# Where the running sums of a decode-attention gradient kernel lie in PSUM, and when its group preparation runs

## The chip, the cores and the metric

The kernel runs on one core of a Trainium2 chip. The metric is the device time of one execution in microseconds (us), taken as the median of several runs. Profiles are of one execution each.

## The reference

A decode step of a transformer block with one token, forward and backward. `x` is a row of 640 elements; it is normalised (`xn`), and attention and a gated MLP are added to it:

```python
x = A_x
xn = _layernorm(x, axis=-1)
return x + _A_ref(xn, A_k_cache, A_v_cache, A_wq, A_wo) + _B_ref(xn, B_w1, B_w3, B_w2)
# _A_ref: q = xn @ wq in 32 heads of 128; p = softmax(q k^T / sqrt(128)) over 8192 keys; (p v) @ wo
# _B_ref: (silu(xn w1) * (xn w3)) @ w2, with 1728 hidden elements
```

The outputs are this row and the gradients, for a given `grad_out`, of x, the K and V caches, wq, wo, w1, w3 and w2. All tensors are bf16. Each head has its own K and V of 8192 x 128, 2 MB each, and gradients dK and dV of the same size, which are outer products of a probability-like column with one row. So nearly all of the 303 MB that move are K and V in, dK and dV out.

## The kernel before

The order of the instructions on every engine is the order of the program text (a manual schedule). The waits between engines are added when the program is built, from which tiles each instruction reads and writes. The tiles of one pool and tag take turns in the buffers of that tag.

The MLP and its gradients come first. Then a loop over the heads (h from 0 to 30; the last head stands behind the loop) treats head c and the head after it, n, in one iteration. The heads lie in 8 groups of 4; `hh` is the place in the group, `g` the group. In one iteration VectorE (DVE) does, in this order:

- `product(n, "S", 0)`: K times q for half of the 128 columns, into a tile T (L403); TensorE (PE) sums T with eight matmuls by the identity into psS (L405);
- `probs(c)`: rZ, the reciprocal of the softmax's sum (L463), and the probabilities;
- `outer(c, ..., "V", 0)`: half of dV into a tile ot, mostly by VectorE (L425), 8 of the 32 columns of a half by ScalarE (ACT, L419);
- `row_dots(c)`, `product(n, "S", 1)`, the other half of dV, then `dscores(c)` (U2, L507) and half of dK;
- `row_max(n)`: reductions of psS (L446, L448);
- `product(n, "DP", 0)`: V times do, in the same manner as S, into psDP; then the other half of dK;
- `exps(n)`: negM, the negated maximum over all rows (L455), and behind it `product(n, "DP", 1)`;
- `weights(c)`: odq (L527), from the head's attention output and dq.

TensorE does the sums of T and several small things: mrow's matmul, which spreads the row maxima over all rows (L450, in `row_max`); `blocks_sum(c)`, eight f32 passes that gather a head's output and dq into two columns, od (L490); rsum's (L459) and rdot's (L503) column sums; on_ps, the group's collected outputs (L538); and the running sums of dxn (L541) and of out (L341, L658), which are added up over all heads.

Two PSUM tiles hold the small results. `accbank` is one tile for the whole kernel, with dxn in columns 0 to 4, out in 5 to 9, on_ps in 16 to 23 and od in 32 to 35. `sm` is a new tile in each head (`row_max`), in a pool with one buffer, with rsum's sum in column 3, rdot's in 4 and the maxima in 8 to 135. `finish_steps` lets ScalarE copy on_ps out (`on_cols`, L332). A third tile, dx_ps, takes dx of the MLP, in three parts of columns; each part is opened with a matmul that has the start flag.

The preparation of the next group, `prep_steps`, is a generator: it turns wo (L292, TensorE), copies it (woT, L297, ScalarE), and makes the broadcast rows q (`qs_g`) and do (`do_g`, L323) of four heads. `gap()` runs one step of the generator that is ahead in `steps`; there are four gaps in an iteration. The generator of the next group is appended at the end of a group's second iteration (hh 1), and the third (hh 2) ends with a fifth gap.

Loads go through SyncE's queue (SP), most stores through GpSimd's (POOL). [...]

Of the kernel before, what the change touches and what calls it, by code (L numbers as in the profile page):

```python
# [10 lines left out]
F32 = mybir.dt.float32  # L11
ALU = mybir.AluOpType
ACTF = mybir.ActivationFunctionType
AX = mybir.AxisListType
PSUM = bass.MemoryType.PSUM

P = 128
# [4 lines left out]
def kernel(  # L22
# [22 lines left out]
    nc = tc.nc  # L45
# [4 lines left out]
    F = B_w1.shape[1]  # L50
# [5 lines left out]
    GH = 4  # L56
# [46 lines left out]
    with tc.manual_schedule(engines=ORDERED):  # L103
# [29 lines left out]
        def turn_lanes(to):  # L133
            k = (to - dealt[0]) % LANES
            if k:
                rows = k if k > 1 else LANES + 1
                nc.gpsimd.dma_start(lane_pad[0:rows, dealt[1] % 2], wq_v[0:rows, 0:2, 0:8])
                dealt[:] = to % LANES, dealt[1] + 1

        def deal(dst, src, p0, p1):  # L140
            nc.gpsimd.dma_start(dst[p0:p1], src[p0:p1])
            dealt[0] = (dealt[0] + (LANES - 1 if p0 == 0 else P - p0)) % LANES
# [79 lines left out]
        nc.vector.memset(accbank[:, 0:16], 0.0)  # L222
        DXN0 = 0
        OUT0 = NC
        OP0 = 16
        OD0 = 32

        sel = consts.tile([P, P // GH], F32, name="sel")
        nc.vector.tensor_reduce(sel[:], ident_f[:].rearrange("p (q r) -> p q r", r=GH), AX.X, ALU.add)
# [50 lines left out]
        def prep_steps(g):  # L280
            G_ = grp[g]
            wq_g, wo_g = G_["wq"], G_["wo"]

            def bank(name, dt, pool=None, tag="w"):
                if g == 0 and pool is not None:
                    return pool.tile([P, GH * DH], dt, name=name, tag=tag)
                return ps_w.tile([P, GH * DH], dt, name=name, tag="w")

            def turn(ci):
                ps_t = bank("ps_t", BF16, ps_o, "ob")  # L290
                for hh in range(GH):
                    nc.tensor.transpose(ps_t[:, hh * DH:(hh + 1) * DH], wo_g[:, hh, ci * P:(ci + 1) * P], ident_bf[:])  # L292
                return ps_t

            def keep(ps_t):
                woT = wpool.tile([P, GH * DH], BF16, name="woT", tag="woT", bufs=3)
                nc.scalar.copy(woT[:], ps_t[:])  # L297
                return woT

            ps_q = bank("ps_q", F32, ps_s, "sm")  # L300
            for ci in range(NC):
                nc.tensor.matmul(ps_q[:], lhsT=xn_col_bf[:, ci:ci + 1].to_broadcast([P, P]), rhs=wq_g[:, ci, :],
                                 start=(ci == 0), stop=(ci == NC - 1))
            yield
            qs_g = wpool.tile([P, GH, DH], BF16, name="qs_g", tag="qs_g")
            nc.scalar.activation(qs_g[:].rearrange("p h d -> p (h d)"), ps_q[:], ACTF.Copy, scale=scale)
            G_["qs"] = qs_g
            ps_t = turn(0)
            yield
            woT = keep(ps_t)  # L310
            ps_t = turn(1)
            yield
            ps_d = bank("ps_d", F32, ps_acc, "acc")
            for ci in range(NC):
                nc.tensor.matmul(ps_d[:], lhsT=g_col_bf[:, ci:ci + 1].to_broadcast([P, P]), rhs=woT[:], start=(ci == 0), stop=(ci == NC - 1))
                if ci + 1 < NC:
                    woT = keep(ps_t)
                if ci + 2 < NC:
                    ps_t = turn(ci + 2)
                if ci not in (2, NC - 1):  # L320
                    yield
            do_g = wpool.tile([P, GH, DH], BF16, name="do_g", tag="do_g")
            nc.scalar.copy(do_g[:].rearrange("p h d -> p (h d)").rearrange("p (q r) -> p r q", r=GH),  # L323
                           ps_d[:].rearrange("p (r q) -> p r q", r=GH))
            G_["do"] = do_g
# [118 lines left out]
        def row_max(st):  # L444
            st.S = small.tile([P, J], F32, name="S_sb", bufs=1)
            nc.vector.tensor_reduce(st.S[:], st.ps["S"][:], AX.X, ALU.add)  # L446
            mrow = small.tile([P, 1], F32, name="mrow")
            nc.vector.tensor_reduce(mrow[:], st.S[:], AX.X, ALU.max)  # L448
            st.sm = ps_s.tile([P, 512], F32, name="sm", tag="sm")
            nc.tensor.matmul(st.sm[:, 8:8 + P], lhsT=mrow[:].to_broadcast([P, P]), rhs=ident_f[:], start=True, stop=True,  # L450
                             skip_group_check=True)

        def exps(st):
            negM = small.tile([P, 1], F32, name="negM")
            nc.vector.tensor_reduce(negM[:], st.sm[:, 8:8 + P], AX.X, ALU.max, negate=True)  # L455
            st.E = small.tile([P, J], F32, name="E", bufs=1)
            rsum = small.tile([P, 1], F32, name="rsum")
            nc.scalar.activation(st.E[:], st.S[:], ACTF.Exp, bias=negM[:], scale=1.0, accum_out=rsum[:])
            nc.tensor.matmul(st.sm[:, 3:4], lhsT=ones_f, rhs=rsum[:], start=True, stop=True, skip_group_check=True)  # L459

        def probs(st):
            rZ = small.tile([P, 1], F32, name="rZ")
            nc.vector.reciprocal(rZ[:], st.sm[:, 3:4])  # L463
            st.P2 = small.tile([P, J, 2], BF16, name="P2")
            nc.vector.tensor_scalar(st.P2[:], st.E[:].unsqueeze(2).to_broadcast([P, J, 2]), rZ[:], None, ALU.mult)
            st.Pf = small.tile([P, 2, ACT_J], F32, name="Pf")
            nc.scalar.activation(st.Pf[:], st.E[:].rearrange("p (a j) -> p a j", a=2)[:, :, JH - ACT_J:JH],  # L467
                                 ACTF.Copy, scale=rZ[:])
# [15 lines left out]

        def blocks_sum(st):
            c0 = OD0 + 2 * (st.h % 2)
            st.od = accbank[:, c0:c0 + 2]
            for r in range(WIDE):
                i, b = divmod(r, WIDE // 2)
                nc.tensor.matmul(st.od, lhsT=st.wide[i][:, b * DH:(b + 1) * DH], rhs=pick[:, r, :],  # L490
                                 start=(r == 0), stop=(r == WIDE - 1), skip_group_check=True)
# [6 lines left out]
        def row_dots(st):  # L498
            st.DP = small.tile([P, J], F32, name="DP_sb", bufs=1)
            nc.vector.tensor_reduce(st.DP[:], st.ps["DP"][:], AX.X, ALU.add)  # L500
            rdot = small.tile([P, 1], F32, name="rdot")
            nc.vector.scalar_tensor_tensor(st.S[:], st.DP[:], 1.0, st.P2[:, :, 0], ALU.mult, ALU.mult, accum_out=rdot[:])
            nc.tensor.matmul(st.sm[:, 4:5], lhsT=ones_f, rhs=rdot[:], start=True, stop=True, skip_group_check=True)  # L503

        def dscores(st):
            st.U2 = small.tile([P, J, 2], BF16, name="U2", bufs=1)
            nc.vector.scalar_tensor_tensor(st.U2[:], st.DP[:].unsqueeze(2).to_broadcast([P, J, 2]), st.sm[:, 4:5], st.P2[:],  # L507
                                           ALU.subtract, ALU.mult)
            st.Uf = None
            if st.h < H - 1:  # L510
                st.Uf = small.tile([P, 2, ACT_J], F32, name="Uf")
                nc.vector.tensor_copy(st.Uf[:], st.U2[:, :, 0].rearrange("p (a j) -> p a j", a=2)[:, :, JH - ACT_J:JH])  # L512
            wide_sums(st.K, st.U2, 1)
# [10 lines left out]
        def weights(st):  # L524
# [9 lines left out]
            om = small.tile([P, GH], F32, name="om")  # L534
            nc.scalar.activation(om[:], rmask[:], ACTF.Copy, scale=odq[:, 0:1])
            if hh == 0:
                G_["on_ps"] = accbank[:, OP0 + GH * (st.g % 2):OP0 + GH * (st.g % 2 + 1)]
            nc.tensor.matmul(G_["on_ps"][hh * (P // GH):(hh + 1) * (P // GH), :], lhsT=sel[:], rhs=om[:],  # L538
                             start=True, stop=True, skip_group_check=True)
            for ci in range(NC):  # L540
# [61 lines left out]
        def dx_part(wi, wt, c0, n):  # L602
            T = tpool.tile([P, n, F], BF16, name="T13", tag="T")
            nc.vector.tensor_tensor(T[:], wt[:, c0:c0 + n, :],
                                    bc_sb[:, wi, :].unsqueeze(1).to_broadcast([P, n, F]), ALU.mult)
            for i in range(F // DR1):
                nc.tensor.matmul(dx_ps[:, c0:c0 + n, :], lhsT=ident_bf[:], rhs=T[:, :, DR1 * i:DR1 * (i + 1)],  # L607
                                 start=(wi == 1 and i == 0), stop=(wi == 0 and i == F // DR1 - 1),
                                 skip_group_check=True)

        def grad(wi, wt):
# [82 lines left out]
        def gap():  # L694
            if steps and next(steps[0], "end") == "end":
                steps.pop(0)

        ob = ps_o.tile([P, 512], F32, name="ob", tag="ob")
        nc.tensor.matmul(ob[:], lhsT=ident_bf[:], rhs=zero_bf[:].to_broadcast([P, WIDE * DH]), start=True, stop=True)
        first = new_head(0)  # L700
# [16 lines left out]
        for h in range(H - 1):  # L717
# [7 lines left out]
            if prev:  # L725
                keep_dq(prev)
            gap()
            row_dots(c)
            attend(c)
            turn_wq(c)  # L730
# [24 lines left out]
            if h == H - 3:  # L755
                for by, dst, src in late:
                    by(dst, src)
                turn_lanes(0)
            gap()
            if n:  # L760
                exps(n)
                product(n, "DP", 1)
            weights(c)
            gap()
            if hh == 1 and g + 1 < NG:
                steps.append(prep_steps(g + 1))
            if hh == 2:
                gap()
            prev = c

        c = hs.pop(H - 1)
# [86 lines left out]
```

## Time and profile before

| | |
|---|---|
| median of 3 runs (lowest to highest) | 720.91 us (719.51 to 721.76) |
| the profiled execution's own time, its span | 720.1 us, 718.3 us |
| mean granted TensorE clock | 0.894 |
| DMA | 303.35 MB, mean 422 GB/s |
| GpSimd busy | 49.5 us (7%) |

On the profile page each engine's busy time stands with its share of the span. Forty equal slices of the span follow, with the busy share in tenths for each engine, the DMA engines' mean busy share and their GB/s. Groups of instructions are named by the line of the kernel, the engine and the operation, with output <- inputs; a bracket or the end of the row has the idle time before them, and what released them. PEld is TensorE's load of weights, which overlaps its matmuls. Matmul ends are modelled.

### The profile page before, as it was taken

The page shows a single profiled execution, that of the slowest core. Times are in us where ns is not written, and L with a number is a line of the kernel's source. Part 1 is how long each engine was busy: PE and PEld are TensorE (multiplying, and loading weights), DVE is VectorE, ACT ScalarE, POOL GpSimd, SP SyncE. Part 2 cuts the span into 40 slices and gives each one's busy share as a digit, 9 for nine tenths or more (in the row PEclk, how much of TensorE's full clock was granted, in tenths as well). Part 3 has the DMA queues.
Part 4 walks back from the last instruction along what each step waited for, and adds up shares of the span by engine and source line. Part 5 has one row for each costly group of instructions (what it writes and reads, how often), then busy time and mean ns, then how long its engine had stood idle before and what let it go on. Part 6 is the DMA issues. An engine that isn't in the chain of part 4 may idle for free.

```text
span 718.3 us, 10242 instructions
## 1 busy us (share of the span) xinstructions
PE 552.2 (77%) x3698; PEld 277.9 (39%) x3698; DVE 630.6 (88%) x722; ACT 479.3 (67%) x1455; POOL 49.5 (7%) x91
## 2 busy tenths in 40 slices
PE   5787788778888797787788787488887878777770
PEld 3653344334444343343343344143443334333330
DVE  5789999899999996798899899499998989999982
ACT  2166666796678856596577866468667957777552
POOL 0010000000000210000000110000000000000100
PEclk9699998997998988799899889889989899999995
DMA  8999999999999999999999999999999999999997
GB/s 354 414 428 425 430 429 430 390 428 428 432 430 429 429 425 426 428 427 429 432 431 428 430 427 424 429 428 427 431 432 428 429 430 430 428 430 431 429 423 309
DMA packets 27696, 303.35 MB, mean 422 GB/s; under 512 B 3264, under 2 KB 3974, under 8 KB 9982
## 3 DMA queue, kind: packets, MB, share of 16 engines
q1 hardware_dynamic: 13490, 154.89, 51.0%
q0 software_dynamic: 10960, 137.72, 45.1%
q10 hardware_dynamic: 3196, 10.10, 3.5%
q8 instruction: 29, 0.48, 0.2%
q14 instruction: 21, 0.17, 0.1%
HBM read 151.34 MB, written 151.34 MB: 421 GB/s over the span
## 4 chain that ended last, share of the span: by engine, by line
DMA 41%; DVE 28%; PE 22%; ACT 5%; issue 1%; SPq 0%; POOL 0%; DVEq 0%; ACTq 0%; POOLq 0%
DMA Kt<-in_A_k_cache_dram 24%; DVE T L403 14%; DMA out_dram<-ot 10%; DVE ot L425 8%; PE ob L474 5%; PE psS L405 5%; PE psDP L405 5%; DMA lane_pad<-in_A_wq_dram 4%; ACT ot L419 3%; DMA Vt<-in_A_v_cache_dram 3%; DMA dbc<-in_B_w_dram 2%; PE accbank L490 1%; DVE DP_sb L500 1%; DVE S_sb L446 1%; PE dx_ps L607 1%
## 5 line engine op out<-in xcount | busy, mean ns | idle before, releaser
L405 PE MATMUL psDP<-T,ident_bf 128*128 128x512 bf16 x512 | 152.2, 451 | 62.1 <-DVE T L403 61.9
L405 PEld LDWEIGHTS <-ident_bf 128*128 128x128 bf16 x1024 | 108.3, 109 | 199.9 <-issue 125.6
L419 ACT ACTIVATE ot<-qs_g,Uf 128x128 bf16<-128x128 bf16 x496 | 151.7, 393 | 41.9 <-DVE Uf L512 26.8
L403 DVE TENSOR_TENSOR T<-Kt,qs_g 128x4096 bf16<-128x4096 bf16 x64 | 146.3, 2286 | 17.4 <-DMA Kt<-in_A_k_cache_dram 16.9
L419 ACT ACTIVATE ot<-do_g,Pf 128x128 bf16<-128x128 bf16 x504 | 153.9, 389 | 1.1
L403 DVE TENSOR_TENSOR T<-Vt,do_g 128x4096 bf16<-128x4096 bf16 x64 | 146.0, 2282 | 2.9 <-ACT do_g L323 1.6
L405 PE MATMUL psS<-T,ident_bf 128*128 128x512 bf16 x512 | 130.2, 400 | 14.9 <-DVE T L403 14.0
L425 DVE TENSOR_TENSOR ot<-qs_g,U 128x3072 bf16<-128x3072 bf16 (+1 forms) x64 | 113.1, 1768 | 13.3 <-DMA out_dram<-ot 13.3
L425 DVE TENSOR_TENSOR ot<-do_g,P 128x3072 bf16<-128x3072 bf16 (+1 forms) x64 | 112.8, 1762 | 6.8 <-DMA out_dram<-ot 5.8
L432 POOL DMA_DIRECT2D out_dram<-ot x60 | 32.2, 537 | 549.9 <-DVE Uf L512 279.3
L474 PE MATMUL ob<-Kt,U 128*4 128x512 bf16 x512 | 60.5, 379 | 1.3 <-DVE U L507 1.3
L474 PE MATMUL ob<-Vt,P 128*4 128x512 bf16 x512 | 61.0, 381 | 0.0
L531 ACT ACTIVATE dq_diag<-ident_bf,odq 128x128 bf16<-128x128 bf16 x32 | 12.8, 401 | 47.2 <-DVE odq L527 47.2
L490 PEld LDWEIGHTS accbank<-pick,wide 128*128 128x128 f32 x256 | 40.1, 223 | 7.8 <-issue 2.4
L467 ACT ACTIVATE Pf<-E,rZ 128x16 f32<-128x16 f32 x32 | 9.8, 305 | 48.4 <-DVE rZ L463 48.4
L297 ACT COPY woT<-ps_t 128x512 bf16<-128x512 bf16 x40 | 23.0, 576 | 21.5 <-PE ps_t L292 21.5
L490 PE MATMUL accbank<-pick,wide 128*128 128x2 f32 x256 | 35.6, 261 | 0.5 <-ACT wide L482 0.5
L450 PE MATMUL sm<-ident_f,mrow 128*128 128x128 f32 x64 | 16.0, 334 | 23.5 <-DVE mrow L448 23.5
L474 PEld LDWEIGHTS <-U 128*4 128x4 bf16 x512 | 19.8, 84 | 36.7 <-DVE U L507 5.2
L474 PEld LDWEIGHTS <-P 128*4 128x4 bf16 x512 | 19.9, 84 | 25.4 <-issue 0.8
L446 DVE TENSOR_REDUCE S_sb<-psS 128x64 f32<-128x512 f32 x32 | 21.9, 685 | 6.0 <-PE psS L405 6.0
L482 ACT COPY wide<-ob 128x256 f32<-128x256 f32 x64 | 19.9, 360 | 8.9 <-PE ob L474 8.9
(165 smaller groups left out, 538.3 us busy)
## 6 DMA issues: line engine op xcount, KB each, us to landing
out_dram<-ot POOLq DMA_DIRECT2D x60, 2048.0 KB, 24.8
Kt<-in_A_k_cache_dram SPq DMA_DIRECT2D x32, 2048.0 KB, 26.4
Vt<-in_A_v_cache_dram SPq DMA_DIRECT2D x32, 2048.0 KB, 21.1
out_dram<-ot SPq DMA_DIRECT2D x8, 1024.0 KB, 13.3
out_dram<-wo_g ACTq DMA_DIRECT2D x6, 640.0 KB, 15.9
wo_g<-in_A_wo_dram ACTq DMA_DIRECT2D x6, 640.0 KB, 15.4
wq<-in_A_wq_dram SPq DMA_DIRECT2D x2, 1280.0 KB, 33.7
w1t<-in_B_w_dram SPq DMA_DIRECT2D x1, 2160.0 KB, 12.3
```

Source lines behind the costliest of these rows:

```text
L297: nc.scalar.copy(woT[:], ps_t[:])
L403: nc.vector.tensor_tensor(T[:], src[:, :, ds_], vec[:, ds_].unsqueeze(1).to_broadcast([P, J, DHH]), ALU.mult)
L405: nc.tensor.matmul(ps[:], lhsT=ident_bf[:], rhs=T[:, :, RUN * i:RUN * (i + 1)], start=(half == 0 and i == 0), stop=(half == 1 and i == DHH ...
L419: nc.scalar.activation(st.ot[half][:, JH - ACT_J + j].rearrange("p a b -> p (a b)"), vec, ACTF.Copy, scale=wf[:, half, j:j + 1])
L425: nc.vector.tensor_tensor(st.ot[half][:, 0:n], vec.rearrange("p (a b) -> p a b", b=2).unsqueeze(1).to_broadcast([P, n, DH // 2, 2]), w2[:, ...
L432: nc.gpsimd.dma_start(dst.rearrange("p j d -> p (j d)"), st.rows[:])
L446: nc.vector.tensor_reduce(st.S[:], st.ps["S"][:], AX.X, ALU.add)
L450: nc.tensor.matmul(st.sm[:, 8:8 + P], lhsT=mrow[:].to_broadcast([P, P]), rhs=ident_f[:], start=True, stop=True, skip_group_check=True)
L474: nc.tensor.matmul(ob[c0:c0 + WIDE, :], lhsT=w2[:, WIDE * q:WIDE * (q + 1), 0], rhs=src[:, WIDE * q:WIDE * (q + 1), :].rearrange("p j d -> ...
L482: nc.scalar.copy(part[:], ob[:, i * (WIDE // 2) * DH:(i + 1) * (WIDE // 2) * DH])
L490: nc.tensor.matmul(st.od, lhsT=st.wide[i][:, b * DH:(b + 1) * DH], rhs=pick[:, r, :], start=(r == 0), stop=(r == WIDE - 1), skip_group_che ...
L531: nc.scalar.activation(dq_diag[:], ident_bf[:], ACTF.Copy, scale=odq[:, 1:2])
```

## The change

The columns of od and on_ps move from `accbank` to `sm`, and `sm` becomes one tile for the whole kernel, allocated ahead of the loop. `accbank` keeps dxn and out alone. dx_ps is opened once, by the first matmul of its first part. In `prep_steps` the steps are cut elsewhere: the copy and matmuls of ci 2, 3 and 4 form the sixth step and the copy into do_g the seventh. The fifth gap moves from the end of the third iteration of a group to the fourth iteration, behind the first gap. The second group's preparation is appended one iteration sooner. A new function, `mark_lanes`, issues eight small loads on GpSimd's queue behind the last turn of the lanes.

```diff
+        def mark_lanes():
+            for i, n in enumerate((3, 5, 6, 7, 9, 10, 11, 12)):
+                r = STRIP + 2 * i
+                nc.gpsimd.dma_start(lane_pad[r:r + 2].rearrange("p a b c -> p (a b c)")[:, 0:n], wq_v[0:2, 0, 0:n])
...
         DXN0 = 0
         OUT0 = NC
-        OP0 = 16
-        OD0 = 32
+        Z0 = 0
+        DOT0 = 1
+        MAX0 = 8
+        OD0 = MAX0 + P
+        OP0 = OD0 + 4
...
-                if ci not in (2, NC - 1):
+                if ci not in (2, NC - 2):
                     yield
...
-            st.sm = ps_s.tile([P, 512], F32, name="sm", tag="sm")
-            nc.tensor.matmul(st.sm[:, 8:8 + P], lhsT=mrow[:].to_broadcast([P, P]), rhs=ident_f[:], start=True, stop=True,
+            nc.tensor.matmul(sm[:, MAX0:MAX0 + P], lhsT=mrow[:].to_broadcast([P, P]), rhs=ident_f[:], start=True, stop=True,
                              skip_group_check=True)
...
-            nc.vector.tensor_reduce(negM[:], st.sm[:, 8:8 + P], AX.X, ALU.max, negate=True)
+            nc.vector.tensor_reduce(negM[:], sm[:, MAX0:MAX0 + P], AX.X, ALU.max, negate=True)
...
-            st.od = accbank[:, c0:c0 + 2]
+            st.od = sm[:, c0:c0 + 2]
...
-                G_["on_ps"] = accbank[:, OP0 + GH * (st.g % 2):OP0 + GH * (st.g % 2 + 1)]
+                G_["on_ps"] = sm[:, OP0 + GH * (st.g % 2):OP0 + GH * (st.g % 2 + 1)]
...
-                                 start=(wi == 1 and i == 0), stop=(wi == 0 and i == F // DR1 - 1),
+                                 start=(wi == 1 and c0 == 0 and i == 0), stop=(wi == 0 and i == F // DR1 - 1),
...
+        sm = ps_s.tile([P, 512], F32, name="sm", tag="sm")
         ob = ps_o.tile([P, 512], F32, name="ob", tag="ob")
...
             gap()
+            if hh == GH - 1:
+                gap()
             row_dots(c)
...
                 turn_lanes(0)
+                mark_lanes()
...
-            if hh == 1 and g + 1 < NG:
+            if hh == (1 if g else 0) and g + 1 < NG:
                 steps.append(prep_steps(g + 1))
-            if hh == 2:
-                gap()
             prev = c
```

The sums of rsum and rdot change their columns in the same way (`Z0` and `DOT0` in place of 3 and 4).

## The prediction

> **What bounds the kernel now.** I read the page's slices first, then VectorE's waits, then the timeline of one head, then the same rows in a head where TensorE ran at half clock.
>
> The slices of the page:
> ```profile
> PE 552.2 (77%) x3698; PEld 277.9 (39%) x3698; DVE 630.6 (88%) x722; ACT 479.3 (67%) x1455; POOL 49.5 (7%) x91
> ...
> DMA  8999999999999999999999999999999999999997
> ```
> The DMA engines are full from the second slice to the last but one, and VectorE (DVE) is busy 88%. Two resources share the bound, so what matters is how often VectorE waits for DMA, since that is the slack in which a new VectorE wait costs nothing. From the waits of VectorE (us in total, times, longest):
> ```profile
> DVE ot L425 <- DMA out_dram<-ot: 19.1, 4, 10.1
> DVE T L403 <- DMA Kt<-in_A_k_cache_dram: 16.9, 12, 4.1
> DVE S_sb L446 <- PE psS L405: 6.0, 5, 2.0
> DVE odq L527 <- PE accbank L490: 5.2, 10, 1.2
> DVE T L403 <- ACT do_g L323: 1.6, 3, 0.6
> DVE T L403 <- DMA Vt<-in_A_v_cache_dram: 1.1, 2, 0.9
> ```
> DMA holds VectorE back for 19.1 + 16.9 + 1.1 = 37.1 us, 1.2 us for each of the 31 loop iterations. That is all the slack there is. Head 4 by the timeline (start, duration, engine and line; in brackets the idle time before, and who ended it):
> ```profile
> 148.81 2.28 DVE L403 TENSOR_TENSOR T<-Vt,do_g 128x4096 bf16<-128x4096 bf16 x1
> 151.01 1.75 DVE L425 TENSOR_TENSOR ot<-qs_g,U 128x3072 bf16<-128x3072 bf16 x1
> 151.15 1.89 PE L405 MATMUL psDP<-T,ident_bf 128*128 128x512 bf16 x8 [1.71 <-DVE T L403]
> 152.68 0.28 DVE L455 TENSOR_REDUCE negM<-sm 128x1 f32<-128x128 f32 x1
> 152.87 0.95 PE L490 MATMUL accbank<-pick,wide 128*128 128x2 f32 x8
> 152.88 2.28 DVE L403 TENSOR_TENSOR T<-Vt,do_g 128x4096 bf16<-128x4096 bf16 x1
> 155.08 0.15 DVE L527 TENSOR_TENSOR odq<-accbank,sc 128x2 f32<-128x2 f32 x1
> 157.09 0.23 PE L538 MATMUL accbank<-om,sel 128*32 128x4 f32 x2
> 157.54 0.16 DVE L463 RECIPROCAL rZ<-sm 128x1 f32<-128x1 f32 x1
> ```
> VectorE runs without a hole here: one head takes 18.7 us from reciprocal to reciprocal. Note that negM (152.68, from `sm`) starts before blocks_sum's matmuls (152.87, into `accbank`) have run. Head 5, the granted clock halved from 170.4 on:
> ```profile
> 169.87 3.06 PE L405 MATMUL psDP<-T,ident_bf 128*128 128x512 bf16 x8 [1.71 <-DVE T L403]
> 171.40 0.28 DVE L455 TENSOR_REDUCE negM<-sm 128x1 f32<-128x128 f32 x1
> 172.72 1.71 PE L490 MATMUL accbank<-pick,wide 128*128 128x2 f32 x8
> 174.71 3.57 PE L405 MATMUL psDP<-T,ident_bf 128*128 128x512 bf16 x8
> 178.32 0.27 PE L538 MATMUL accbank<-om,sel 128*32 128x4 f32 x2
> ```
> The same eight psDP matmuls take 3.57 us for 1.89, and blocks_sum ends 3.03 us after negM's start instead of 1.14.
>
> **The part that decides: od and on_ps move into `sm`.** The waits between engines are made from the program, by PSUM tile and not by column. The program of before has two such waits: ScalarE's copy of on_ps (L332) waits for the last of L541's matmuls, which writes other columns of `accbank`; and L538's matmul carries a wait for VectorE's read of od (L527), also other columns. The latter stands in the trace, one event in each head:
> ```profile
> L538 PEldq EVENT_SEMAPHORE  x32: 51/51/51, 77.3 to 700.0; - x32
> ```
> After the change mrow's matmul, od, rsum's sum, on_ps and rdot's sum are columns of one tile, so a read by VectorE waits for the last TensorE write into any of them that stands ahead of it in program order. By that order:
>
> 1. negM (L455) follows blocks_sum and must wait for it. Behind it in VectorE's queue stand T of the second DP half, odq, T of the next head: everything. Price: from negM's start to the end of L490's last matmul. Read off the timeline iteration by iteration, that is 1.14 us in 19 of the 31 and 2.26 to 3.54 us (mean 2.76) in 12, where the clock was halved or the step began late: 19 x 1.14 + 12 x 2.76 = 54.8 us. I add 0.03 us each time for the step between the engines (in head 5 L490 ends at 174.43 and odq, which waits for it, starts at 174.46), 0.9 us. The 5.2 us that odq waits for L490 today fall inside. Net 50.5 us.
> 2. rZ (L463) follows on_ps's matmul (L538) and must wait for it. At full clock L538 ends at 157.32, 0.22 us before rZ: hidden by T of the next head. At half clock psDP is 1.68 us longer, so the wait is about 1.68 - 0.22 = 1.46 us (in head 5 L538 ends at 178.59, 1.67 us after rZ). None in any head would be 0, all heads 31 x 1.46 = 45 us. Today L538 ends after rZ in 10 iterations, 15.3 us in sum. After the change TensorE idles longer between blocks_sum and the second DP half (2.3 us of negM and T, against 1.4 between 153.82 and 155.22 in head 4), which makes half clock there more frequent; I take 15 heads, 22 us.
> 3. odq (L527) must wait for rsum's matmul (L459). It ended before odq in most heads, and T (2.28 us) covers it: nothing; up to 3.2 us once, in head 10, where ScalarE was late.
> 4. rdot's matmul (L503) waits for ScalarE's on_cols (L332) in the first head of a group, behind eight ot copies of 2.45 us. Queued behind it is attend. VectorE has its own 1.75 us outer product in between; 7 heads, 0 to 0.5 us each, taken at nothing.
>
> `accbank`, left with sums that nothing reads until L804, costs nothing and gains nothing. Opening dx_ps once changes a flag on matmuls and no count.
>
> The Trainium skill, "PSUM — Partial Sum Buffer", "Summary: rules for kernel authors", says to read PSUM while a matmul runs only from a different bank; before keeps this rule for negM against blocks_sum, the change breaks it. By that rule alone the price is the same as under 1.
>
> **Preparation.** Today the fifth step directly follows the fourth at the end of a group's third head. ScalarE's in-order queue then stands 3.90 us at 116.23 for ps_t before Pf, and in the fourth head VectorE loses 1.71 us on S_sb (128.54) and 0.60 us on do_g. The move puts two steps with three 0.58 us copies and two sets of transposes (0.38 us) ahead of rdot instead; TensorE and ScalarE alternate there, some 0.5 us a turn. At most the whole 6.0 + 1.6 us of these waits goes; at worst U waits about 1 us more in 6 groups. I take -1 us. The second group a head sooner moves the same instructions to heads 1 and 2; no DMA moves, its wo was loaded at the start.
>
> **mark_lanes.** Eight DMA issues on GpSimd's queue behind the last lane_pad one at 670.4; at its 0.95 us each 7.6 us, on a queue that holds nothing afterwards. Like their forerunner (landing in 25.8 to 38.8 us) they land by about 717, before the end of 718.3. Nothing, with a bound of 1 us.
>
> **The sum.** VectorE's path gets 50.5 + 22 - 1 = 71.5 us longer. It gives back the 37.1 us of DMA waits, as DMA then has time to catch up, and part of the tail: the last K half is computed at 701.9 and the span ends 16.4 us later, since stores of 1 MB take 13.3 us to land behind a backlog; with an empty queue I estimate 6 us less. 71.5 - 37.1 - 6 = +28.4. The profiled execution took 720.1 us (span 718.3, 1.8 outside): 748.5, and the median of the runs lies 0.8 above it: **749 us**.
>
> **Rivals.**
> - *DMA hides it* (not slower). The slack of 1.2 us a head is just the full-clock price, 1.14 + 0.03. If TensorE stays at full clock in nearly all heads, DMA stays the bound: 720 to 727 us. It decides as long as VectorE's average loss is under about 1.2 us a head. For it: slices of 428 to 430 GB/s throughout. Against: 12 slow heads in 31. 0.10.
> - *No such waits* (the regrouping of PSUM does not add them, by columns being told apart). Then preparation alone is left: 719 us, since DMA hides most of it. Against: L332 and L538 above. 0.07.
> - *The clock feeds back.* More idle time, more half clock. If all heads went at half clock: 31 x 2.8 - 5 + 45 - 43 = +84, 804 us; half of that extra gives 777. For it: four of the first five half-clock stretches of the loop (91.92, 112.40, 170.43 and 228.45) begin within 1.4 us of the start of a first DP half, right behind an idle time of TensorE. Against: most stretches end within 7 us. 0.15 for over 770. The Trainium skill, "TensorE: Matmul & The Clock Gate", "Part 1: The HAM clock gate", says that an idle window of about 3.4 us halves the clock; the trace agrees on the length, since the stretches are multiples of 3.41 us (91.92 to 95.33), and shows them after partly idle windows too: the stretch from 112.40 follows 3.41 us in which psDP's matmuls had run since 111.06.
>
> **Numbers.** My case has 0.68, with its own range 735 to 770. The range 724 to 786 takes in part of the first rival and most of the third. 0.3%, or 2.2 us, is about what a measurement of this kernel can tell from no change; the second rival lies half on that line, the first mostly within or above. Faster 0.05, same 0.09, slower 0.86.
>
> **What would show it.** Right: in VectorE's waits a new row of negM for L490, about 50 us, in nearly every head; a row of rZ for L538, 10 to 35 us; the waits for out_dram and Kt under 10 us; DMA slices at 400 to 415 GB/s; no change in the matmul counts; eight more lane_pad issues. Wrong: no idle time before negM, or idle time there with the DMA slices still full and DMA waits still about 37 us.

## The result, and the profile after

The changed kernel takes 773.05 us (median of 4 runs, 768.90 to 777.51) against 720.21 us (719.36 to 721.76): ratio 1.073, interval 1.067 to 1.080. That is 53 us more; 749 was forecast, with a range of 724 to 786. The profiled execution of the changed kernel, the longest of the four, took 777.51 us; its span is 775.6 us, 57.3 us above the 718.3 of before. Its lines are renumbered: negM is L462 (was L455), blocks_sum L497 (L490), rZ L470 (L463), on_ps's matmul L545 (L538), T L411 (L403), psDP's and psS's matmuls L413 (L405), ot L433 (L425), rdot L510 (L503), on_cols L340 (L332).

The page's busy times, the granted clock, the DMA engines' slices and rates, and the shares of the chain that ended last:

```profile
PE 592.1 (76%) x3698; PEld 291.5 (38%) x3698; DVE 633.8 (82%) x722; ACT 480.9 (62%) x1455; POOL 53.6 (7%) x99
...
PEclk9689998879888779898889779998979779978795
DMA  8999989999989999999989999999989999999956
GB/s 355 420 422 433 424 323 387 396 373 387 410 326 416 420 407 425 409 423 428 430 325 419 419 392 420 414 428 427 426 341 411 414 385 388 363 406 373 407 232 238
...
DVE 56%; PE 36%; ACT 3%; issue 2%; DMA 2%; SPq 0%; DVEq 0%; ACTq 0%
```

The instruction counts of TensorE, VectorE and ScalarE are those of before, and VectorE does the same work (633.8 us for 630.6). But DMA has fallen from 41% to 2% of the chain that sets the end, and the rates have holes of 323 to 341 GB/s; over the loop they average 396, for 428 before (400 to 415 in the slices was forecast). The bound is now VectorE together with TensorE. VectorE's waits say where:

```profile
DVE negM L462 <- PE sm L497: 58.5, 31, 3.0
DVE rZ L470 <- PE sm L545: 42.8, 31, 3.5
...
DVE S_sb L454 <- PE psS L413: 3.4, 7, 2.0
DVE odq L534 <- PE sm L497: 3.2, 1, 3.2
```

Two rows that did not exist before, each in all 31 iterations, 101.3 us in sum. Every row with a wait for Kt, Vt or out_dram is gone: the 37.1 us of DMA waits were given back in full. The timeline of iteration 1, which answers to head 4 of before:

```profile
96.32 1.75 DVE L433 TENSOR_TENSOR ot<-qs_g,U 128x3072 bf16<-128x3072 bf16 x1
96.45 1.89 PE L413 MATMUL psDP<-T,ident_bf 128*128 128x512 bf16 x8 [1.71 <-DVE T L411]
...
98.17 0.95 PE L497 MATMUL sm<-pick,wide 128*128 128x2 f32 x8
...
99.16 0.29 DVE L462 TENSOR_REDUCE negM<-sm 128x1 f32<-128x128 f32 x1 [1.09 <-PE sm L497]
99.37 2.28 DVE L411 TENSOR_TENSOR T<-Vt,do_g 128x4096 bf16<-128x4096 bf16 x1
...
101.57 0.15 DVE L534 TENSOR_TENSOR odq<-sm,sc 128x2 f32<-128x2 f32 x1
101.71 3.38 PE L413 MATMUL psDP<-T,ident_bf 128*128 128x512 bf16 x8 [1.34 <-DVE T L411]
...
105.07 0.22 PE L545 MATMUL sm<-om,sel 128*32 128x4 f32 x2
...
105.33 0.17 DVE L470 RECIPROCAL rZ<-sm 128x1 f32<-128x1 f32 x1 [1.22 <-PE sm L545]
```

negM no longer starts beside blocks_sum but 0.04 us after its last matmul has ended (98.17 + 0.95 = 99.12). The first DP half ran at full clock (1.89 us), the second mostly at half clock (3.38 us). From the end of blocks_sum (99.12) to the start of the second half (101.71) TensorE stood idle for 1.95 us (0.61 and 1.34), against 1.01 (0.52 and 0.49) in head 4 of before; whether that is the reason, e9 tests below. So on_ps's matmul is late, and rZ waits 1.22 us for it. In iteration 8 both halves ran slowly:

```profile
250.97 3.06 PE L413 MATMUL psDP<-T,ident_bf 128*128 128x512 bf16 x8 [1.71 <-DVE T L411]
...
253.83 1.71 PE L497 MATMUL sm<-pick,wide 128*128 128x2 f32 x8
...
255.57 0.29 DVE L462 TENSOR_REDUCE negM<-sm 128x1 f32<-128x128 f32 x1 [2.99 <-PE sm L497]
...
258.12 3.57 PE L413 MATMUL psDP<-T,ident_bf 128*128 128x512 bf16 x8 [1.14 <-DVE T L411]
...
261.99 0.17 DVE L470 RECIPROCAL rZ<-sm 128x1 f32<-128x1 f32 x1 [1.47 <-PE sm L545]
```

An iteration takes 21.2 us in the first case and 23.4 in the second; head 4 of before took 18.7. By the timelines of all 31 iterations, half clock touches the first DP half in 15 of them (12 before) and the second in all 31 (12 before).

From the first rZ to the last the loop grew from 629.8 to 687.5 us, +57.6. The terms by VectorE's waits in the loop: 58.5 + 42.8 new; 37.1 of DMA, 4.0 of odq for L490, 2.7 of S_sb and 1.6 of do_g gone; +55.9. VectorE's own instructions take 3.1 us longer there (576.1 us for 573.0), and 1.4 us of smaller differences stay. The stretch ahead of the loop is 2.6 us longer, the one behind it 2.9 us shorter.

### The profile page after: what moved, and what is told of

Same layout as the page of the kernel before. It is cut to its first block, busy times and chain, and to the rows that moved or that the text cites. A ratio compares the mean times of both kernels' runs of the same rounds, so it can differ in the third digit from the quotient of the medians.

```text
span 775.6 us, 10248 instructions
## 1 busy us (share of the span) xinstructions
PE 592.1 (76%) x3698; PEld 291.5 (38%) x3698; DVE 633.8 (82%) x722; ACT 480.9 (62%) x1455; POOL 53.6 (7%) x99
## 3 DMA queue, kind: packets, MB, share of 16 engines
q1 hardware_dynamic: 13490, 154.89, 50.5%
## 4 chain that ended last, share of the span: by engine, by line
DVE 56%; PE 36%; ACT 3%; issue 2%; DMA 2%; SPq 0%; DVEq 0%; ACTq 0%
DVE T L411 26%; PE psDP L413 24%; DVE ot L433 17%; PE sm L497 4%; DVE S_sb L454 3%; DVE DP_sb L507 2%; ACT ot L427 2%; PE ob L481 2%; PE psS L413 2%; DMA dbc<-in_B_w_dram 2%; DVE negM L462 1%; DVE P L472 1%; DVE U L514 1%; ACT woT L305 1%; PE dx_ps L614 1%
## 5 line engine op out<-in xcount | busy, mean ns | idle before, releaser
L413 PE MATMUL psDP<-T,ident_bf 128*128 128x512 bf16 x512 | 186.2, 530 | 88.7 <-DVE T L411 88.7
L413 PEld LDWEIGHTS <-ident_bf 128*128 128x128 bf16 x1024 | 114.5, 115 | 230.1 <-issue 170.2
L411 DVE TENSOR_TENSOR T<-Kt,qs_g 128x4096 bf16<-128x4096 bf16 x64 | 146.2, 2285 | 1.1 <-PE psDP L413 1.1
L411 DVE TENSOR_TENSOR T<-Vt,do_g 128x4096 bf16<-128x4096 bf16 x64 | 146.0, 2282 | 0.0
L413 PE MATMUL psS<-T,ident_bf 128*128 128x512 bf16 x512 | 126.6, 392 | 1.0 <-DVE T L411 1.0
L433 DVE TENSOR_TENSOR ot<-do_g,P 128x3072 bf16<-128x3072 bf16 (+1 forms) x64 | 112.9, 1763 | 1.1
L433 DVE TENSOR_TENSOR ot<-qs_g,U 128x3072 bf16<-128x3072 bf16 (+1 forms) x64 | 113.2, 1768 | 0.0
L462 DVE TENSOR_REDUCE negM<-sm 128x1 f32<-128x128 f32 x32 | 9.3, 291 | 58.5 <-PE sm L497 58.5
L538 ACT ACTIVATE dq_diag<-ident_bf,odq 128x128 bf16<-128x128 bf16 x32 | 12.9, 402 | 58.4 <-DVE odq L534 58.4
L465 ACT ACTIVATE E<-S_sb,negM 128x64 f32<-128x64 f32 x32 | 11.1, 348 | 59.9 <-DVE negM L462 59.8
L497 PEld LDWEIGHTS sm<-pick,wide 128*128 128x128 f32 x256 | 44.5, 246 | 9.0 <-issue 4.1
L470 DVE RECIPROCAL rZ<-sm 128x1 f32<-128x1 f32 x32 | 5.4, 168 | 42.8 <-PE sm L545 42.8
L497 PE MATMUL sm<-pick,wide 128*128 128x2 f32 x256 | 39.6, 277 | 0.5 <-ACT wide L489 0.5
L466 PE MATMUL sm<-rsum,ones_fc 128*128 128x1 f32 x64 | 14.4, 294 | 24.5 <-ACT E L465 24.5
## 6 DMA issues: line engine op xcount, KB each, us to landing
Kt<-in_A_k_cache_dram SPq DMA_DIRECT2D x32, 2048.0 KB, 18.7
wo_g<-in_A_wo_dram ACTq DMA_DIRECT2D x6, 640.0 KB, 16.4
```

Of the source, the lines that this page charges most:

```text
L411: nc.vector.tensor_tensor(T[:], src[:, :, ds_], vec[:, ds_].unsqueeze(1).to_broadcast([P, J, DHH]), ALU.mult)
L413: nc.tensor.matmul(ps[:], lhsT=ident_bf[:], rhs=T[:, :, RUN * i:RUN * (i + 1)], start=(half == 0 and i == 0), stop=(half == 1 and i == DHH ...
L433: nc.vector.tensor_tensor(st.ot[half][:, 0:n], vec.rearrange("p (a b) -> p a b", b=2).unsqueeze(1).to_broadcast([P, n, DH // 2, 2]), w2[:, ...
L462: nc.vector.tensor_reduce(negM[:], sm[:, MAX0:MAX0 + P], AX.X, ALU.max, negate=True)
L466: nc.tensor.matmul(sm[:, Z0:Z0 + 1], lhsT=ones_f, rhs=rsum[:], start=True, stop=True, skip_group_check=True)
L538: nc.scalar.activation(dq_diag[:], ident_bf[:], ACTF.Copy, scale=odq[:, 1:2])
```

## The experiments

The theory was: VectorE's reads of `sm` wait for every earlier TensorE write into that tile in program order, and TensorE's half clock makes these waits longer. Rivals: the other parts of the change (preparation, marks) carry some of the loss; the shared tile costs whatever the order; the half clock has nothing to do with TensorE's idle time at these places.

**Both columns back (e1), on_ps back (e2), od back (e3), the move alone (e4).** Three put columns back on the changed kernel, the fourth does the move alone on the kernel before.

```diff
 e1, e2:  -                G_["on_ps"] = sm[:, OP0 + ...
          +                G_["on_ps"] = accbank[:, OP0 + ...       (OP0 = 16)
 e1, e3:  -            st.od = sm[:, c0:c0 + 2]
          +            st.od = accbank[:, c0:c0 + 2]                (OD0 = 32)
 e4, on the kernel before: one sm for all heads, with od in columns 136 to 139 and on_ps from 140 on
```

> The changed kernel, with od and on_ps in accbank again as in the kernel before (columns 32 and 16); the one permanent sm, the single opening of dx_ps, the new preparation steps and the marks stay. Theory (waits by PSUM tile carry the whole loss): 718 to 722 us, no wait of negM for blocks_sum and none of rZ for on_ps, and the 37 us of waits for DMA come back. Rival (the preparation steps or the marks carry part of it): 730 us or more.

Measured: 721.35 us, ratio 1.0014 (1.0000 to 1.0029), and neither new row is left; VectorE waits 44.7 us for DMA again. The preparation steps and the marks, which this kernel has, cost at most 0.3% while DMA is the bound.

> The changed kernel, with on_ps alone in accbank again; od stays in sm. Theory: the 42.8 us of rZ's waits are gone, negM's wait stays at 45 to 58 us, and since VectorE's path is then only some 10 to 20 us above what DMA needs, part is hidden: 725 to 742 us. If instead negM's wait alone makes the loss and rZ's wait only moved to where another wait would have been, 760 us or more.

Measured: 745.23 us over four runs (740.29 to 752.66), 742.32 without the longest, which the ratio leaves out: 1.032 (1.026 to 1.037). That is just above the range of the theory and far under the rival's. The waits, in an execution of 748.14 us:

```profile
DVE negM L462 <- PE sm L497: 51.6, 31, 3.5
DVE T L411 <- DMA Vt<-in_A_v_cache_dram: 12.1, 2, 6.7
DVE T L411 <- DMA Kt<-in_A_k_cache_dram: 11.0, 3, 4.5
```

rZ's row is gone, negM's is nearly whole. What the expectation missed is the second and third row: with 51.6 us more on VectorE's path, 23.1 us of waits for DMA stay, in five long ones. They lie in two places, between 325 and 360 us and between 503 and 527. So the slack of 37.1 us can't be spent anywhere in the loop; why these two places keep their waits is not shown. Half clock touches the second DP half in 29 of the 31 iterations here, where on_ps is out of `sm` and negM still waits.

> The changed kernel, with od alone in accbank again; on_ps stays in sm. Theory: the 58.5 us of negM's waits are gone; rZ's wait stays, but smaller than 42.8 us (15 to 35 us), because TensorE no longer idles for negM ahead of the second DP half and so runs less at half clock; DMA's slack of 37 us hides nearly all of it: 719 to 727 us. If the clock at that place does not depend on negM's wait, rZ's wait stays at 40 us or more and the time is 725 to 735 us.

Measured: 724.91 us, 1.006 (1.004 to 1.008).

```profile
DVE rZ L470 <- PE sm L545: 12.5, 9, 3.4
```

rZ's wait is below even the lower figure, and half clock touches the second DP half in 12 iterations, as before. So most of rZ's 42.8 us exist only because negM waits.

> The kernel before with one thing changed: od and on_ps in one permanent sm. Old preparation steps, dx_ps opened three times, no marks. Theory: the whole loss is here, 770 to 780 us, up to 5 us above the changed kernel, as the old steps cost a little more where VectorE is the bound. Rival (preparation or marks carry part): 765 us or less.

Measured: 769.26 us (768.23 to 772.33), 1.068 (1.065 to 1.071), with negM's wait at 56.4 us and rZ's at 37.1. That is 0.7 us below the range expected and well above the rival's. The move alone makes the whole loss, as far as these runs can tell: the interval overlaps that of the changed kernel. It is no slower than the changed kernel, against the expectation that the old steps cost a little more.

**Reads ahead of writes (e5, e10).** The same grouping of columns, but in another program order: negM's reduction stands ahead of blocks_sum(c), and on_ps's matmul of a head behind rZ of the next.

```diff
-            blocks_sum(c)
             outer(c, c.q, c.U2, c.Uf, "K", h, 1)
+            if n:
+                neg_max(n)
+            blocks_sum(c)
...
             probs(c)
+            if prev:
+                collect(prev)
```

> The changed kernel with the same grouping of the columns (od and on_ps in the one sm, dxn and out alone in accbank), but two writes stand behind the reads they delayed in program order: negM's reduction comes ahead of blocks_sum, and on_ps's matmul of a head comes behind the next head's rZ. Each engine's own order stays, but for on_ps's matmul, which TensorE now does behind eight psS matmuls. Theory (a read waits for every earlier write to its tile in program order, and for nothing else): the waits of 58.5 and 42.8 us vanish, 718 to 723 us, and the waits for DMA are back at 30 to 40 us. Rival (the shared tile itself costs, whatever the order: blocks_sum now waits for negM's read, and odq is late by it): 730 us or more, with odq's wait at 20 us or more.

Measured: 721.48 us, 1.0022 (1.0011 to 1.0032). Its waits:

```profile
DVE T L411 <- DMA Kt<-in_A_k_cache_dram: 15.5, 11, 3.6
DVE ot L433 <- DMA out_dram<-ot: 14.5, 3, 9.8
DVE odq L536 <- PE sm L468: 11.8, 12, 4.1
```

Both rows of 58.5 and 42.8 us have vanished with every column where the change put it. odq now waits 11.8 us for rsum's matmul (L468), its last predecessor in `sm`; the time shows next to nothing of it, as VectorE still waits 33.5 us for DMA. e10 does the same on the kernel before, with the old preparation steps and no marks:

> The kernel before with the new grouping in PSUM, dx_ps opened once, negM's reduction ahead of blocks_sum and on_ps's matmul behind the next head's rZ in program order; old preparation steps, no marks. Theory: the grouping costs nothing in this order, 718.5 to 721.5 us, the kernel before within 0.3%. Rival (rsum's sum, which odq must wait for, delays VectorE: 11.8 us of odq's waits were seen with the new steps): 723 to 728 us.

Measured: 720.09 us, 1.0001 (0.9989 to 1.0013). The grouping and the single opening of dx_ps cost nothing that these runs can tell in this order, and no version here is faster than the kernel before.

**TensorE kept busy (e6, e9, e11, e12).** Zero matmuls fill TensorE's idle time on the changed kernel.

```diff
+        def fill(k):
+            for _ in range(k):
+                nc.tensor.matmul(ob[:], lhsT=ident_bf[:], rhs=zero_bf[:].to_broadcast([P, WIDE * DH]), start=True, stop=True,
+                                 skip_group_check=True)
...
                 row_max(n)
+                fill(FILL)        # e6 alone
                 product(n, "DP", 0)
             blocks_sum(c)
+            fill(FILL)            # e6, e9, e11, e12; FILL = 6
```

> The changed kernel with six matmuls of 128x512 more (zeros into ob, which is opened anew anyway) in each head at two places where TensorE idles: behind mrow's matmul, ahead of the first DP half, and behind blocks_sum, ahead of rsum. They fill 1.3 us at full clock, of 1.7 and 2.4 us of idle time. Theory (half clock follows from these idle times, and makes the waits longer): the granted clock rises from 0.84 to 0.95 or more, negM's wait falls from 58.5 to 35 to 40 us (1.1 us a head) and rZ's from 42.8 to under 15 us: 725 to 740 us. Rival (the clock does not depend on these places, or the added matmuls delay as much as they gain): 770 us or more, clock below 0.88.

Measured: 743.01 us, 1.031 (1.027 to 1.035), clock 0.96; rZ's wait fell to 1.9 us, but negM's only to 53.3, not to 35 to 40, and the time is above the 740 of the theory. The row of the added matmuls says why, here in the worst head:

```profile
152.21 0.49 PE L458 MATMUL sm<-ident_f,mrow 128*128 128x128 f32 x2 [0.16 <-DVE mrow L457]
...
153.72 0.61 ACT L495 COPY wide<-ob 128x256 f32<-128x256 f32 x2
154.27 1.75 DVE L434 TENSOR_TENSOR ot<-qs_g,U 128x3072 bf16<-128x3072 bf16 x1
154.39 2.37 PE L463 MATMUL ob<-zero_bf,ident_bf 128*128 128x512 bf16 x6 [1.69 <-ACT wide L495]
...
156.55 2.71 PE L414 MATMUL psDP<-T,ident_bf 128*128 128x512 bf16 x8
```

The ones ahead of the first DP half write `ob`, which ScalarE was still reading; they waited, and psDP started 2.28 us after its T (154.27 is when VectorE went on to ot). By the timeline this delayed psDP in 13 of the 31 heads, by 0.7 to 2.2 us. The experiment made a new wait of the kind under study. e9 leaves those out:

> The changed kernel with six zero matmuls of 128x512 in each head, now only behind blocks_sum, into ob; those ahead of the first DP half are left out, as they had to wait for ScalarE's copy of ob. Theory (half clock at the second DP half comes from TensorE's idle time while VectorE does negM and T): the half clock share in the loop falls from 0.30 to about 0.2, rZ's wait from 42.8 to 5 to 20 us, and negM's to 45 to 58 us, as the first DP half stays as it was: 740 to 755 us. Rival (only the total of TensorE's work sets the clock, not the place): rZ's wait stays above 30 us, 765 us or more.

Measured: 746.84 us, 1.036 (1.033 to 1.040). In the profile, of the fastest of the four runs (742.11 us), half clock fills 8% of the loop (after: 30%, before: 20%):

```profile
DVE negM L468 <- PE sm L503: 51.7, 31, 3.5
...
DVE rZ L476 <- PE sm L551: 1.9, 1, 1.9
```

The time is in the range of the theory; the clock and rZ's wait fell further than it said. Half clock touches the second DP half in 2 iterations, for 31. Six matmuls that compute nothing make the kernel 26 us faster, and 40.9 us of rZ's wait went with the half clock. e11 puts six more ahead of the first DP half, into psDP itself:

> As before, six zero matmuls behind blocks_sum, and six more ahead of the first DP half into the psDP tile that the half opens anew, which waits for nobody. Theory: TensorE stays at full clock in nearly all heads; negM's wait falls to 31 times 1.1, about 35 us, rZ's below 5 us, the same 37 to 40 us as the slack that DMA leaves: 722 to 730 us, with waits for DMA of some us back. Rival (the waits depend on the order alone and not on the clock): negM's wait stays above 50 us, 740 us or more.

Measured: 724.42 us, 1.005 (1.003 to 1.007). In this kernel six more stand ahead of the second DP half too and put zeros over the sums of the first, so its dK and dwq are not the reference's. e12 has the six only ahead of the first half, where nothing is lost:

```diff
             st.ps[which] = ps_acc.tile([P, J, RUN], F32, name="ps" + which, tag="acc")
+            if which == "DP" and half == 0:
+                fill(FILL, st.ps[which][:].rearrange("p j r -> p (j r)"))
```

> The changed kernel with six zero matmuls of 128x512 behind blocks_sum (into ob) and six ahead of the first DP half alone (into psDP, which that half opens anew). In the run before this one six more stood ahead of the second DP half by an oversight. Theory: those made no difference to the waits that matter; half clock in the loop under 0.05, negM's wait 35 to 40 us, rZ's below 5 us, 722 to 728 us. Rival (the third set kept TensorE at full clock): rZ's wait back at 10 us or more, 732 us or more.

Measured: 724.43 us, 1.005 (1.003 to 1.007); half clock in 1% of the loop:

```profile
DVE negM L471 <- PE sm L506: 37.6, 31, 2.8
DVE ot L436 <- DMA out_dram<-ot: 7.1, 2, 5.1
DVE T L414 <- DMA Kt<-in_A_k_cache_dram: 4.2, 3, 1.9
...
DVE rZ L479 <- PE sm L554: 1.9, 1, 1.9
```

negM still waits in all 31 iterations, 1.1 us in most, 1.2 in the mean: that is the wait that the order makes. The other 58.5 - 37.6 = 20.9 us of negM's wait and nearly all of rZ's came with the half clock.

**Preparation and marks (e7, e8).** On the changed kernel, the old cut of the steps, and no mark_lanes.

```diff
 e7:  -                if ci not in (2, NC - 2):
      +                if ci not in (2, NC - 1):
      (the fifth gap back to the end of hh 2; the second group's steps appended at hh 1)
 e8:  -                mark_lanes()
```

> The changed kernel with the preparation steps of the kernel before (the fifth gap at the end of a group's third head, the second group's steps in its old place, the copy of ci 4 in the last step). VectorE is the bound here, so what these steps cost VectorE is seen in the time. By the prediction (the new steps gain 1 us, at most 7.6): 773 to 780 us. Rival (the new steps cost, as two steps ahead of rdot hold TensorE): 767 to 771 us, like the kernel with the move alone.

> The changed kernel without mark_lanes. By the prediction nothing waits for these eight loads: within 1 us of the changed kernel, 772 to 774 us. Rival (their waits on GpSimd's queue or their small packets delay the last stores): 765 to 770 us.

Measured: e7 769.51 us (766.01 to 773.20), 1.069 (1.066 to 1.072); e8 771.84 us (767.00 to 773.72), 1.071 (1.069 to 1.074). e7's median lies in its rival's range, 767 to 771, and e8's 0.2 us below the range expected. But both intervals overlap that of the changed kernel, 1.067 to 1.080, so neither part has an effect that these runs tell apart, and e7's rival, that the new steps cost some us, is not excluded. In e7's profile the waits for do_g are back at 4.3 us, but negM and rZ wait 12.5 us less than in the changed kernel's profile (55.1 + 33.7 against 58.5 + 42.8). The new steps do what they should at do_g, and nothing of it can be seen in the time. Half clock fills 26% of e7's loop, for 30%; whether the new steps cause the difference stays open, as the comparison is of one profile each.

## Why the prediction was right

The waits that it named came, in the heads and at the rows that it named, and they make the loss. Its size was not right: +53 us against +28 forecast. The time is outside the main case's own range, 735 to 770; the range 724 to 786 holds it because that takes in most of the rival *the clock feeds back*, which came to pass in part. The mechanism, step by step:

- *negM waits for blocks_sum*: right in place, count and size. 55.7 us gross was priced, 58.5 measured (16 iterations at 1.10 us, 15 at 2.5 to 3.0). e3 takes it away by the tile, e5 by the order.
- *rZ waits for on_ps's matmul*: right in place, and the term that was mis-sized: 22 us priced, 42.8 measured, also above the 10 to 35 us given as a sign of being right. The price per wait (1.46 us) held: 42.8 / 31 = 1.38. The count did not: 15 heads were assumed, it was all 31. The step that failed is the estimate of how often the second DP half runs at half clock. It was raised from 10 to 15 by the longer idle time, but that idle time stands in every head, and half clock touched the second half in all 31. e2 (29 heads, negM waiting), e3 (12, negM's wait gone) and e9 (2, the idle time filled) show the link.
- *odq*: 4.0 of its 5.2 us, nine waits, fell inside negM's wait as priced. The tenth stands behind the loop, in the last head, where no negM goes ahead of it: 1.2 us before, 3.2 after, still for blocks_sum. For rsum's matmul it waits nowhere, as priced.
- *rdot waits for on_cols*: it does, for 10.9 us over the 7 heads in the row of its weight loads, longest 1.9, not 0 to 0.5 each; at VectorE, dscores has no wait behind it, so the price of nothing held.
- *The waits for DMA are given back*: all 37.1 us were, here. e2 shows that the step is not general: there 23.1 us of waits for DMA stood although VectorE lost 51.6.
- *The tail*: -6 us was priced, an estimate without a row behind it, and -2.9 measured. The median store of 1 MB lands in 5.8 us for 13.3, and from the last K half (764.1) to the end of the span it takes 11.5 us for 16.4, 4.9 less. But from the last rZ to that half it takes 2.0 us more, by odq's longer wait.
- *Preparation* (-1 us) *and marks* (nothing): nothing that can be told apart. Of the 6.0 us of S_sb's waits that the new steps were to take away at most, 2.0 stand ahead of the loop, out of their reach. The issues of the marks were priced wrongly: they stand on GpSimd's queue from 723.6 to 740.6, 17 us for 7.6, with 12.6 us of waits for stores to land. The last of them landed well before the end, so the price of nothing held. The 2.6 us ahead of the loop were not foreseen; the first rZ comes at 59.9 to 63.2 us over all the kernels here, e1's at 60.2 with the same code there, so scatter between executions can explain it.

In the loop, then, +34.4 us was priced (50.5 + 22 - 1 - 37.1) and +57.6 measured; 20.8 of the 23.2 between are rZ's.

Of the rivals, *no such waits* fell with the two new rows. *DMA hides it* was priced at 720 to 727 us for a TensorE at full clock: e12 made that condition, and took 724.43. (The slices that it read as 428 to 430 GB/s throughout are 414 to 432 on the page of before, with one of 390 and the first and last lower.) *The clock feeds back* was right in kind and came about halfway: the share of half clock in the loop rose from 0.20 to 0.30, and about 62 of the 101 us of waits (20.9 + 40.9) are its work. It should not have stood as a rival to the main case; it was a part of it. In e9 and e12 matmuls on zeros lowered the half clock share to 0.08 and 0.01. The Trainium skill's rule in "TensorE: Matmul & The Clock Gate", "Part 1: The HAM clock gate", that an idle window lowers the clock and sustained work raises it, agrees with that in direction. But here the window need not be idle: all 35 half clock stretches that begin in the loop of the changed kernel follow 3.41 us in which TensorE was busy for 36 to 73%, and its longest idle time there was 1.71 us.

## What to carry to other kernels

When small results are regrouped in PSUM, list for each tile the reads and writes in program order: a read waits for the last write ahead of it to any column, so a read that used to run beside another engine's writes must be moved ahead of them in the program, which cost nothing here (e10). Price a new wait together with the idle time that it makes on the other engine, since the clock of TensorE answers to it. And slack that shows as waits for DMA is not spent freely: under 101 us of new waits all 37 us of it came back, under 51.6 us (e2) the waits for DMA fell only by 14.

## What the runs showed of the hardware

TensorE's half clock can be bought off with work that is thrown away: 12 matmuls on zeros a head (378 more in all) made the changed kernel 49 us faster (773.05 to 724.43), although each took TensorE's time. And TensorE need not stand still to lose its clock. In the loops of both kernels half clock came in stretches of 3.41 us or whole multiples of it. With both loops cut into stretches of 3.41 us, none in which TensorE was busy for less than 49% (by the profile's matmul times) was followed by full clock, and some in which it was busy for as much as 74% were followed by half clock.
